# A long S4 and expert-layer kernel on one core: whole rows in one stage of the taps' transform, one product on another engine, and later transposes

## The chip, the cores and the metric

The kernel runs on one core of a Trainium2 chip. The metric is the device time of one execution in microseconds (us). Several executions are timed; one more is recorded by the hardware profiler, and all rows of the profile are from that one.

## The reference

The input x has 2048 rows of 576 channels. The output mixes two branches with a gate for each row:

```python
g = sigmoid((x * gate_w).sum(-1, keepdims=True))
return g * a + (1 - g) * b
# a: K = einsum(C, exp(dt*A*l), dt*B).real      128 states for each of 576 channels
#    a = irfft(rfft(pad(x)) * rfft(pad(K)))[:2048] + x * Dskip
# b: q = x . w_q (32 heads);  s1 = q1 . k1,  s2 = q2 . k2  (64 keys each)
#    the best 2 of each, the best 2 of their 4 sums, softmax -> weights p of 2 experts e for each head
#    b = sum over heads and experts of p * gelu(x . u[e]) * v[e]     (4096 experts)
```

Branch a is a long convolution, done by Fourier transforms; its "taps" are K. Branch b is a layer of experts chosen by product keys.

## The kernel before, in words

One Python program writes the instructions of all engines. While it writes, it keeps a clock of its own with a cost for each instruction; pieces of work are generators that wait on that clock ("ready", "need") and are resumed by a queue ("spawn", "pump"). So the order of the instructions on each engine is fixed when the program is built. It follows from the costs and from the order in which the generators become ready.

TensorE (PE) has two long kinds of work, drawn by the main loop from two lists: 128 "s" groups (scores of one part of the heads `c` for one tile `t` of 128 rows; named s5_0 and so on) and 128 "a" groups (x . u for part `c`; named a6_1_0). Each fills one PSUM bank. A group is written in one of two ways. In `halved` it is 27 matmuls on 64 rows of the array, the upper half rows first and the lower ones later in the same bank; `row_slot` writes one upper half of a group beside one lower half of an earlier group, and the two run side by side. In `triple` it is 14 matmuls on all 128 rows. `start_group` chooses; before, it takes `triple` only if the quota of score banks, `caps["sc"]`, is under 4.

The eight PSUM banks are shared by tags with quotas: "sc" for the groups, "wb" and "kb" for all else. `quota(...)` sets them at each stage.

Between the groups come the stages of the convolution. The first part makes the taps and stores them (`k_gen`, `k_store`, to k_d in HBM). When the last are stored, `freq` starts. It loads the tables tk and the stored taps (ksb, four DMAs), and then does, in this order:

- `k_stage1`: 32 steps, k1_0 to k1_31. Each has two banks (k1_w_0, k1_w_1) of 288 columns, two copies to k1o (four buffers) and one store to sk_d. Before, each bank is 4 half matmuls.
- beside it `v_norm` (loads vn in quads, products on GpSimd, sums of squares vj on ScalarE; at its end a small matmul pvn) and `gating(c)` for the parts of the heads (the softmax weights; tiles ggu, ggd, ggi, ggib; results in vals).
- `products`: 36 steps that load ui and ki back from su_d and sk_d, transform them (matmuls pr, pi), multiply them (tt, vf on VectorE and GpSimd), transform back (pv, vo) and store.
- at the end of `gating(7)` the transposes tr0 to tr15 of vals; then the one-hot matrices and sums S (`prep`), the table vhl of the experts' v, and the output stage, matmuls o.

wn and wb are the small sums and products that build the next part's key weights. Nearly all DMAs are issued by SyncE (SP), in the order in which they are written. In the profile nearly all instructions of an engine have one line (L216 for matmuls, L136 for the other engines, L207 for DMAs), so tiles tell them apart.

Of the kernel before, what the change touches and what calls it, by code (L numbers as in the profile page):

```python
# [140 lines left out]
def body(ctx: ExitStack, tc: tile.TileContext, xT, au, par, logdt, dskip, gatew, wq, kT, uT, vv,  # L141
# [5 lines left out]
    clock = [0.0]  # L147
# [106 lines left out]
                    g["then"]()  # L254

    chained = [False]

    def total(p, cols):

# [752 lines left out]
    def k_store(c, kb):  # L1012
        yield from ready(kb)
        yield from need("ko")
        take("ko", "ko")
        ko = kg.tile([128, 2, 2 * NI * R2], F16, name="ko", tag="ko", bufs=1)
        kq = kb.rearrange("p (c i q) -> p q c i", c=2, i=NI)
        kz = ko.rearrange("p z (q c i) -> p z q c i", c=2, i=NI)
        S.activation(kz[:, 0], kq, AF.Copy)
        yield from ready(ko)  # L1020
        V.tensor_sub(kz[:, 1], kq, kz[:, 0])
        free("kb", ko, of=kb)
        yield from ready(ko)
        kstored[0] += 2
        dma(k_d[c].rearrange("p z m q -> p z (m q)"), ko)
        free("ko", k_d)
        if kstored[0] == NCK:
            while uf != 0:
                yield 0.3
            KG.__exit__(None, None, None)  # L1030
            quota(sc=5, wb=4, kb=0, raw=2)
            spawn(freq())


# [78 lines left out]
    def gating(c):  # L1113

        while taken[c] < 4 or not ff:
            yield 0.5
        vv_ = vals[:, :, 8 * c:8 * c + 8].rearrange("p t (h s) k -> p t h s k", s=2)
        ii = idx[:, :, 8 * c:8 * c + 8].rearrange("p t (h s) k -> p t h s k", s=2)
        tl = lambda nm, *z: ff.tile([128, NT, 4, *z], F32, tag="gg" + nm, name=f"gg{nm}{c}")
        a0, a1, b0, b1 = vv_[:, :, :, 0, 0], vv_[:, :, :, 0, 1], vv_[:, :, :, 1, 0], vv_[:, :, :, 1, 1]  # L1120
        u, w, s, d = tl("u"), tl("w"), tl("s"), tl("d")
        i1, i2, ib = tl("i1", 2), tl("i2", 2), tl("ib", 2)
        G.tensor_add(u, a0, b1)
        G.tensor_add(w, a1, b0)
        G.tensor_add(d, a0, b0)
        yield from ready(u, w)
        V.tensor_tensor(out=s, in0=u, in1=w, op=OP.is_ge)
        V.tensor_tensor(out=u, in0=u, in1=w, op=OP.max)
        yield from ready(u, d)
        G.tensor_sub(d, u, d)  # L1130
        db = d.rearrange("p (b t) h -> p b (t h)", b=4)
        G.tensor_mul(db, db, i_x[:, :, None].to_broadcast([128, 4, 16]))
        dx = d.rearrange("p t (x y) -> p t x y", x=2)
        G.tensor_mul(dx, dx, invW[:, None, 2 * c:2 * c + 2, None].to_broadcast([128, NT, 2, 2]))
        yield from ready(d)
        S.activation(d, d, AF.Exp)
        yield 1
        G.tensor_sub(w, ii[:, :, :, 1, 1], ii[:, :, :, 1, 0])
        G.tensor_mul(w, w, s)
        G.tensor_add(i2[:, :, :, 1], ii[:, :, :, 1, 0], w)  # L1140
        yield 2
        G.tensor_sub(w, ii[:, :, :, 0, 0], ii[:, :, :, 0, 1])
        G.tensor_mul(w, w, s)
        G.tensor_add(i1[:, :, :, 1], ii[:, :, :, 0, 1], w)
        S.activation(i1[:, :, :, 0], ii[:, :, :, 0, 0], AF.Copy)
        S.activation(i2[:, :, :, 0], ii[:, :, :, 1, 0], AF.Copy)
        yield from ready(i1, i2, d)
        V.tensor_scalar(ib, i2, 0.5, -0.25, op0=OP.mult, op1=OP.add)
        V.tensor_scalar(ib, ib, MAGIC, MAGIC, op0=OP.add, op1=OP.subtract)
        V.scalar_tensor_tensor(i1, i2, 64.0, i1, op0=OP.mult, op1=OP.add)  # L1150
        fl = lambda x: x.rearrange("p t h k -> p t (h k)")
        V.scalar_tensor_tensor(place[0][:, :, 8 * c:8 * c + 8], fl(ib), -128.0, fl(i1), op0=OP.mult, op1=OP.add)
        S.activation(place[1][:, :, 8 * c:8 * c + 8], fl(ib), AF.Copy)
        V.tensor_scalar(u, d, 1.0, None, op0=OP.add)
        V.reciprocal(u, u)
        V.tensor_scalar(u, u, 2.0 ** 14, None, op0=OP.mult)
        pr = prob[:, :, 8 * c:8 * c + 8].rearrange("p t (h k) -> p t h k", k=2)
        yield from ready(u)
        S.activation(pr[:, :, :, 0], u, AF.Copy)
        G.tensor_mul(pr[:, :, :, 1], u, d)  # L1160
        if c < 7:
            spawn(gating(c + 1))
            return
        gated.append(1)
        yield from ready(vals)
        for t in range(NT):
            yield from need("wb")
            p = bank("wb", f"tr{t}")
            for r, x, i in ((0, place[0][:, t], identb), (1, place[1][:, t], identb), (2, prob[:, t], ident)):
                for hh in range(2):  # L1170
                    mm(p[64 * hh:64 * hh + 64, 64 * r:64 * r + 64], x, i[:, 64 * hh:64 * hh + 64], True, True,
                       0.12 if r == 2 else 0.04)
            spawn(turned(t, p))
            del p
# [91 lines left out]
    def k_stage1(ksb, fk, tabs):  # L1266
        enter, leave, count = ring(3)

        def tail(w, o, pbs, gs):
            while not all(g["done"] for g in gs):  # L1270
                yield 0.2
            yield from ready(*pbs)
            for hh in range(2):
                copy(o[:, 288 * hh:288 * hh + 288], pbs[hh][:, :288])
                free("wb", o, of=pbs[hh])
            yield from ready(o)
            dma(pair_rows(sk_d, w), o)
            leave(w)

        for w in range(32):  # L1280
            tkt = tabs[w // 16]
            yield from ready(tkt, ksb)
            yield from enter()
            o = fk.tile([128, D], F32, tag="s1o", name=f"k1o{w}", bufs=4)
            pbs, gs = [], []
            yield from need("wb", 2)
            for hh in range(2):
                pb = bank("wb", f"k1_{w}_{hh}")
                pbs.append(pb)
                gs.append(rows(*([(pb[:, :288], tkt[h:h + 64, w % 16, n],  # L1290
                                   ksb[h:h + 64, 2 * hh:2 * hh + 2, :, w, :].rearrange("p j c i -> p (j c) i"),
                                   h == 0 and n == 0, h == 64 and n == 1) for n in range(2)] for h in (0, 64)), first=True))
            spawn(tail(w, o, pbs, gs))
            del pb, pbs
        while count() < 32:
            yield 0.5
# [102 lines left out]
    def freq():  # L1399
        nonlocal ff, ab, iota_a, iota_b  # L1400
        ff = FG.__enter__()
        wrems.append(ff.tile([128, 2, 512], F16, name="wrem3"))
        ksb = KS.__enter__().tile([128, 4, NCK // 2, 32, 2 * NI], F16, name="ksb")
        fk = FK.__enter__()
        tabs = [fk.tile([128, 16, 2, 128], F16, tag="tk", name=f"tk{w0}", bufs=2) for w0 in (0, 16)]
        for w0, tkt in zip((0, 16), tabs):
            dma(tkt, tk_d[:, w0:w0 + 16, :])
        for j in range(4):
            while wire[0] > clock[0] + 2:
                yield 0.3  # L1410
            dma(ksb[:, j].rearrange("p c w i -> p c (w i)"),
                k_d[:, 32 * j:32 * j + 32].rearrange("c l z m n -> (l z m) c n"))
        spawn(v_norm(), 4)
        spawn(gating(0), 20)
        yield from k_stage1(ksb, fk, tabs)
        FK.__exit__(None, None, None)
        KS.__exit__(None, None, None)
        v_pool(0, 3)
        spawn(v_work())
        fp = FP.__enter__()  # L1420
        quota(sc=4, wb=5)
        yield 3
        spawn(prep(0))
        yield from products(fp)
        FP.__exit__(None, None, None)
        quota(sc=4, wb=4)
        ab = ctx.enter_context(tc.tile_pool(name="ab", bufs=1, side="right"))
        iota_a = ab.tile([128, 128, 2], F16, name="iota_a")
        iota_b = ab.tile([128, 64, 2], F16, name="iota_b")
        V.tensor_copy(iota_a, cst[:, 384:512, None].to_broadcast([128, 128, 2]))  # L1430
        V.tensor_copy(iota_b, cst[:, 512:576, None].to_broadcast([128, 64, 2]))
        iotas.append(1)
        v_pool(3, 5)
        while not gated or not gates:
            yield 0.5
        FG.__exit__(None, None, None)
        WJ.__exit__(None, None, None)
        v_pool(5, 8)
        shut.append(1)
# [447 lines left out]
    def start_group(g):  # L1887

        x = xb[tb_of(g)]
        if len(g) == 2:  # L1890
            c, t = g
# [21 lines left out]
                spawn(act_post(c, tb, j, pb))  # L1913
                used(("u", c), ("x", tb))
        parity[0] = tb_of(g) % 2
        if caps["sc"] < 4:
            while upper or lower:
                row_slot()
            chained[0] = False
# [120 lines left out]
```

## Time and profile before

| | us |
|---|---|
| median of 3 runs | 1452.51 |
| lowest to highest | 1450.69 to 1454.05 |
| profiled execution | 1452.08 |
| its span | 1450.3 |
| PE busy in the span | 1421.3 (98%) |
| VectorE (DVE) busy | 1192.9 (82%) |
| ScalarE (ACT) busy | 831.2 (57%) |
| GpSimd (POOL) busy | 478.1 (33%) |

The page's first part gives busy time by engine. A window is a stretch of the span with the busy time of each engine in it. A row of the waits names the engine and tile that waited, what released it, the time in total, how often, and the longest wait. In a timeline a row is one instruction or several alike (xN), with its start, its length, and in brackets the idle time before it. In the shapes, 64\*128 is a matmul on half the array's rows, 128\*128 on all.

### The profile page before, as it was taken

What the parts mean: (1) busy time and instruction counts of PE and PEld (TensorE: products, weight loads), DVE (VectorE), ACT (ScalarE), POOL (GpSimd) and SP (SyncE); (2) the same over time, 40 slices, a digit from 0 to 9 for tenths busy, and PEclk for the clock granted to TensorE, in tenths of its full rate; (3) what the DMA queues carried; (4) which work ended last, traced back from release to release, by engine and by line L of the source; (5) the groups of instructions that cost most, each with busy time, mean ns of one, the idle gap of its engine ahead of it and who ended that gap; (6) DMA issues with size and microseconds to landing.
All of it is one profiled execution on the core that took longest, in us unless ns stands there. A gap on an engine that the chain in (4) does not pass through costs nothing.

```text
span 1450.3 us, 43981 instructions
## 1 busy us (share of the span) xinstructions
PE 1421.3 (98%) x17654; PEld 904.7 (62%) x17654; DVE 1192.9 (82%) x4596; ACT 831.2 (57%) x1445; POOL 478.1 (33%) x488
## 2 busy tenths in 40 slices
PE   7999999999999999999999999999999999999998
PEld 3465567554565665455654444446888788888887
DVE  5887699889889988777789987688988889889870
ACT  6547887987888887664656665563423422332230
POOL 0443265552572663530557899400000000000000
PEclk9999999999999999999999999999999999999999
DMA  9333543343351331238785788687342432541410
GB/s 315 117 110 99 167 134 111 99 129 109 111 157 47 120 104 46 78 125 269 252 274 168 258 275 305 211 269 235 112 137 82 155 120 71 174 129 68 144 52 17
DMA packets 134380, 215.89 MB, mean 149 GB/s; under 512 B 10912, under 2 KB 79904, under 8 KB 127776
## 3 DMA queue, kind: packets, MB, share of 16 engines
q1 hardware_dynamic: 134080, 213.01, 45.3%
q8 instruction: 138, 2.26, 0.7%
q14 instruction: 66, 0.54, 0.1%
q10 hardware_dynamic: 96, 0.07, 0.0%
HBM read 141.74 MB, written 71.30 MB: 147 GB/s over the span
## 4 chain that ended last, share of the span: by engine, by line
PE 90%; DMA 4%; DVE 4%; ACT 1%; issue 1%; SPq 0%; POOL 0%; ACTq 0%; DVEq 0%; POOLq 0%
PE o L216 26%; PE a L216 25%; PE s L216 23%; PE S L216 4%; PE kb L216 2%; PE pr L216 2%; PE wb L216 2%; DMA wq<-in_wq_dram 1%; PE kP L216 1%; PE y L216 1%; DVE i L136 1%; PE pv L216 1%; PE u L216 1%; DVE m L136 1%; DMA ki<-sk_d 1%
## 5 line engine op out<-in xcount | busy, mean ns | idle before, releaser
L216 PE MATMUL s<-whl,xb 64*128 64x512 f16 x3072 | 468.9, 377 | 0.6 <-ACT k1o L136 0.4
L216 PE MATMUL a<-xb,uhl 64*128 64x512 f16 (+1 forms) x3024 | 455.4, 376 | 0.5 <-DVE go L136 0.2
L216 PE MATMUL o<-vhl,wh 128*128 128x288 f16 x3072 | 387.5, 286 | 0.0
L216 PEld LDWEIGHTS <-wh 128*128 128x128 f16 x3072 | 295.8, 98 | 76.1 <-issue 3.7
L216 PEld LDWEIGHTS <-xb 64*128 64x128 f16 x3456 | 227.8, 94 | 165.7 <-issue 14.5
L216 PEld LDWEIGHTS <-uhl 64*128 64x128 f16 (+1 forms) x3024 | 196.3, 94 | 164.9 <-issue 7.4
L136 ACT ACTIVATE wh<-gl,s_wg 128x1024 f16<-128x1024 f32 x64 | 68.8, 1137 | 180.2 <-DVE gl L136 180.2
L136 POOL TENSOR_TENSOR CS<-CS,ex 128x512 f32<-128x512 f32 x72 | 90.7, 1293 | 167.1 <-DVE ex L136 167.1
L136 DVE TENSOR_TENSOR gl<-S,gl 128x256 f32<-128x256 f32 x256 | 90.9, 416 | 48.5 <-PE S L216 26.2
L216 PE MATMUL s<-wrem,xb 64*128 64x512 f16 x384 | 122.1, 376 | 0.0
L216 PE MATMUL a<-xb,wrem 64*128 64x512 f16 (+1 forms) x380 | 120.0, 376 | 0.0
L136 ACT ACTIVATE go<-a,i_a 128x512 f32<-128x512 f32 x99 | 67.6, 684 | 85.7 <-PE a L216 61.4
L136 DVE FIND_INDEX8 i<-m,s 128x8 uint32<-128x64 f32 x520 | 104.9, 223 | 0.0
L136 POOL TENSOR_TENSOR e<-aN,rt 128x512 f32<-128x512 f32 x72 | 84.0, 1186 | 47.1 <-PE kb L216 47.0
L136 DVE FIND_INDEX8 i<-m,sx 128x8 uint32<-128x64 f32 x504 | 99.4, 218 | 0.0
L136 DVE MAX8 m<-s 128x8 f32<-128x64 f32 x520 | 74.4, 215 | 27.0 <-PE s L216 22.8
L136 ACT ACTIVATE gl<-gl 128x1024 f32<-128x1024 f32 x64 | 63.1, 1046 | 47.0 <-DMA gl<-g_d 47.0
L136 DVE TENSOR_TENSOR Bg<-Be,vals 128x1024 f16<-128x1024 f16 x128 | 82.8, 688 | 2.2
L136 DVE SCALAR_TENSOR_TENSOR wh<-gl,s_wg,wh 128x1024 f16<-128x1024 f32 x64 | 78.5, 1279 | 0.9 <-ACT wh L136 0.9
L136 ACT ACTIVATE CS<-CS 128x1024 f32<-128x1024 f32 x72 | 74.6, 1049 | 6.3 <-DVE CS L136 6.1
L136 DVE TENSOR_TENSOR A<-iota_a,vals 128x2048 f16<-128x2048 f16 x64 | 77.8, 1216 | 0.0
L136 DVE MAX8 m<-sx 128x8 f32<-128x64 f32 x504 | 69.4, 209 | 5.4 <-ACT sx L136 5.1
(206 smaller groups left out, 2360.8 us busy)
## 6 DMA issues: line engine op xcount, KB each, us to landing
g_d<-go SPq DMA_DIRECT2D x128, 256.0 KB, 2.6
gl<-g_d SPq DMA_DIRECT2D x32, 1024.0 KB, 7.0
wq<-in_wq_dram SPq DMA_DIRECT2D x16, 1152.0 KB, 6.0
su_d<-us SPq DMA_DIRECT2D x32, 288.0 KB, 2.6
sk_d<-k1o SPq DMA_DIRECT2D x32, 288.0 KB, 2.7
ui<-su_d SPq DMA_DIRECT2D x16, 576.0 KB, 4.1
ki<-sk_d SPq DMA_DIRECT2D x16, 576.0 KB, 5.8
vn<-in_vv_dram SPq DMA_DIRECT2D x32, 288.0 KB, 4.5
```

Of the source, the lines that this page charges most:

```text
L136: return f(*a, **k)
L216: return T.matmul(o, l, r, start=start, stop=stop)
```

## The change

It has three parts. In the taps' first stage, `start_group` writes whole-row groups and `k_stage1` writes two whole matmuls for a bank in place of four halves; "phase" tells where the program is, and the quota of score banks is 4 there, not 5. In `gating(7)` the last product goes to VectorE; the other parts' stays on GpSimd. And the transposes start to be written once the program's clock is 2 us past the point at which vals is ready.

```diff
     chained = [False]
+    phase = ["taps"]
...
-            quota(sc=5, wb=4, kb=0, raw=2)
+            quota(sc=4, wb=4, kb=0, raw=2)
+            phase[0] = "k1"
             spawn(freq())
...
-        G.tensor_mul(pr[:, :, :, 1], u, d)
+        (V if c == 7 else G).tensor_mul(pr[:, :, :, 1], u, d)
...
-        yield from ready(vals)
+        yield from ready(vals, late=2.0)
...
                 pbs.append(pb)
+                if not chained[0]:
+                    for n in range(2):
+                        mm(pb[:, :288], tkt[:, w % 16, n], ksb[:, 2 * hh:2 * hh + 2, :, w, :].rearrange("p j c i -> p (j c) i"),
+                           n == 0, n == 1)
+                    continue
...
         quota(sc=4, wb=5)
+        phase[0] = "products"
...
         quota(sc=4, wb=4)
+        phase[0] = "last"
...
-        if caps["sc"] < 4:
+        if clock[0] < 0 or phase[0] in ("k1",):
             while upper or lower:
                 row_slot()
             chained[0] = False
```

In `start_group` the lines that follow (`triple`, `then`, return) stay. `chained` also decides how the wn sums are written (`total`): whole or halved. Since the order follows from costs, all engines' order changes from here on.

On PE, at the first step of the stage, before: k is k1_0, s_7 and s_8 are groups s5_7 and s5_8, each weight load ahead of its matmul. One upper and one lower half alternate.

```order
11332 L216 MATMUL s_7_11590<-whl_10645,xb_146 128x512
11333 L216 LDWEIGHTS tk_11205
11334 L216 MATMUL k_0_1_11717<-ksb,tk_11205 128x288
11335 L216 LDWEIGHTS xb_146
11336 L216 MATMUL s_7_11590<-whl_10645,xb_146 128x512
11337 L216 LDWEIGHTS tk_11205
11338 L216 MATMUL k_0_1_11717<-ksb,tk_11205 128x288
```

The same place on PE now. The eight matmuls of k1_0 (two banks of two halves each, upper and lower) are four, and stand together.

```order
11114 L216 MATMUL s_7_11585<-whl_10645,xb_146 128x512
11115 L216 LDWEIGHTS tk_11205
11116 L216 MATMUL k_0_0_11596<-ksb,tk_11205 128x288
11117 L216 LDWEIGHTS tk_11205
11118 L216 MATMUL k_0_0_11596<-ksb,tk_11205 128x288
11119 L216 LDWEIGHTS tk_11205
11120 L216 MATMUL k_0_1_11599<-ksb,tk_11205 128x288
11121 L216 LDWEIGHTS tk_11205
11122 L216 MATMUL k_0_1_11599<-ksb,tk_11205 128x288
11123 L216 LDWEIGHTS xb_146
```

What moved: 15 s groups, s5_0 to s5_14, and all of k1 are whole now, and bank 0 of a step comes before bank 1. Further on, pr0 stands after s5_15, s6_0 and s6_4, and no longer after s6_1, s6_5, the uppers of s6_2 and wb7_0.

On SP, the end of the stage before (sk_d is a store of the stage, vn a quad of v_norm's loads, wq the next weights, ui and ki the loads of the first products):

```order
258 L207 DMA vn_12786<-in_au_dram 32x576 x4
259 L207 DMA sk_d<-k1o_12708 32x4x576
260 L207 DMA wq_0_12839<-in_wq_dram 128x2304
261 L207 DMA sk_d<-k1o_12741 32x4x576
262 L207 DMA vn_12884<-in_au_dram 32x576 x4
263 L207 DMA sk_d<-k1o_12769 32x4x576
264 L207 DMA ui_12961<-su_d 128x1152
265 L207 DMA ki_12962<-sk_d 128x1152
```

The end of the stage on SP now:

```order
255 L207 DMA sk_d<-k1o_12216 32x4x576
256 L207 DMA sk_d<-k1o_12229 32x4x576
257 L207 DMA vn_12291<-in_au_dram 32x576 x4
258 L207 DMA sk_d<-k1o_12247 32x4x576
259 L207 DMA ui_12345<-su_d 128x1152
260 L207 DMA ki_12346<-sk_d 128x1152
261 L207 DMA ui_12349<-su_d 128x1152
262 L207 DMA ki_12350<-sk_d 128x1152
263 L207 DMA vn_12353<-in_au_dram 32x576 x4
264 L207 DMA wq_0_12415<-in_wq_dram 128x2304
```

What moved: eight vn quads, not twelve, stand between the first and the last store, and the wq load stands behind the first two pairs of ui and ki.

On VectorE, the end of gating 7 and the first results of the transposes before (vhl is a step of the experts' table, vo a copy of a product's result):

```order
972 L136 TENSOR_SCALAR ggu_15729<-ggu_15729 128x64
973 L136 COPY vo_16092<-pv_0_16093 128x128
974 L136 SCALAR_TENSOR_TENSOR vhl_12897<-vhl_12898,sci,vhl_12897 128x576 x2
975 L136 COPY vo_16092<-pv_0_16176 128x256
976 L136 SCALAR_TENSOR_TENSOR vhl_12897<-vhl_12898,sci,vhl_12897 128x576 x2
977 L136 SCALAR_TENSOR_TENSOR vhl_12898<-vhl_12899,sci,vhl_12898 128x576 x2
978 L136 TENSOR_TENSOR vals<-tr_16268,vals 128x64
```

The same piece of VectorE now:

```order
965 L136 TENSOR_SCALAR sc<-pvn 128x1
966 L136 TENSOR_SCALAR sci<-sc 128x1
967 L136 TENSOR_SCALAR sci<-sci 128x1 x2
968 L136 TENSOR_SCALAR ggib_15480<-ggi_15479 128x128
...
974 L136 TENSOR_SCALAR ggu_15474<-ggu_15474 128x64
975 L136 CAST iota_a<-cst 128x256
976 L136 CAST iota_b<-cst 128x128
977 L136 TENSOR_TENSOR vals<-ggu_15474,ggd_15477 128x16x4
978 L136 TENSOR_TENSOR vals<-tr_15892,vals 128x64
```

What moved: pvn's scale now comes directly ahead of gating 7 (before it stood among the products, ahead of their last copies), the product and the iota casts are between gating and the transposes, and the vhl steps come after the first transposes. On PE pvn now stands behind the last product pv_35, and 57 half matmuls of a groups lie between pvn and tr0. On ScalarE a vhl step stands between the copies of tr0 and tr1. On PE the blocks S15_0 to S15_2 all come ahead of the first o matmul; before, S15_2 came after it.

## The prediction

> **What bounds the kernel now.** I read the page first, then the windows by stage, then what the TensorE (PE) waits for. The page gives the length and PE's share, and one group from which a price comes:
>
> ```profile
> span 1450.3 us, 43981 instructions
> ...
> PE 1421.3 (98%) x17654; PEld 904.7 (62%) x17654; DVE 1192.9 (82%) x4596; ACT 831.2 (57%) x1445; POOL 478.1 (33%) x488
> ...
> L216 PE MATMUL o<-vhl,wh 128*128 128x288 f16 x3072 | 387.5, 286 | 0.0
> ```
>
> PE is busy for 98% of the span. The change can therefore win little by giving PE less work elsewhere; it can win the last idle stretches of PE, or lose by opening new ones. The windows show where they lie: the columns are length, then busy time of PE, PEld, DVE, ACT and POOL, the granted clock and the DMA share.
>
> ```profile
> 651.00:685.10 34.10, 31.68 (x399) 16.74 (x399) 24.58 (x177) 14.75 (x31) 0.00 (x0) 1.00 0.92 282
> 685.10:735.50 50.40, 47.14 (x516) 35.15 (x518) 36.77 (x250) 31.87 (x100) 28.16 (x51) 0.97 0.74 242
> 735.50:748.50 13.00, 11.65 (x157) 8.50 (x152) 12.69 (x107) 6.27 (x19) 6.26 (x14) 1.00 0.82 268
> 748.50:894.50 146.00, 143.24 (x1793) 68.75 (x1791) 131.01 (x804) 91.09 (x256) 121.79 (x151) 1.00 0.74 250
> 894.50:919.50 25.00, 24.35 (x297) 11.33 (x295) 19.33 (x37) 16.32 (x41) 24.06 (x29) 1.00 0.81 283
> 919.50:994.70 75.20, 75.20 (x843) 36.88 (x840) 56.57 (x97) 42.47 (x71) 3.31 (x3) 1.00 0.70 230
> 994.70:1450.30 455.60, 451.96 (x5249) 365.30 (x5248) 368.33 (x612) 134.77 (x137) 0.00 (x0) 1.00 0.35 112
> ```
>
> The second row is the first stage of the taps' transform (k1), the fourth and fifth the products, the last the output. From 651 to 919.5 PE is idle for 34.10 + 50.40 + 13.00 + 146.00 + 25.00 less 31.68 + 47.14 + 11.65 + 143.24 + 24.35, which is 10.4 us. That is the pool for this change. PE's waits name the pieces (total, times, longest):
>
> ```profile
> PE k L216 <- ACT k1o L136: 2.8, 4, 1.1
> PE k L216 <- DVE m L136: 2.5, 1, 2.5
> PE pr L216 <- DMA ki<-sk_d: 1.5, 1, 1.5
> PE wn L216 <- ACT wj L136: 1.4, 2, 0.9
> PE wn L216 <- ACT tt L136: 1.1, 1, 1.1
> ```
>
> **Whole rows cost nearly what halves cost.** Two pieces of PE's timeline: a run of half matmuls (two rows that follow one another) and a run of whole ones.
>
> ```profile
> 951.65 2.32 PE L216 MATMUL a<-xb,uhl 64*128 64x512 f16 x20
> 953.80 0.38 PE L216 MATMUL a<-xb,wrem 64*128 64x512 f16 x1
> ...
> 23.65 1.03 PE L216 MATMUL a<-xb,wrem 128*128 128x512 f16 x4
> 24.51 1.03 PE L216 MATMUL a<-xb,uhl 128*128 128x512 f16 x4
> ```
>
> Twenty halves start over 953.80 - 951.65 = 2.15 us, two in 0.215 us. Four whole ones take 24.51 - 23.65 = 0.86 us, one in 0.215. A group is 27 halves, 13.5 x 0.215 = 2.90 us, or 14 whole, 3.01 us. Fifteen groups change: 15 x 0.11 = 1.6 us more. An o matmul of the k1 shape takes 387.5 / 3072 = 0.126 us, so the 128 whole k1 matmuls are 16.1 us. This work is not new time by itself, since what ends the stage is another matter: the chain through the store.
>
> TensorEngine Tiling (Array Packing) of the Trainium skill, Key Properties, says that a change of tiling mode drains the engine. By that the whole rows would add drains where the halves end and begin again; the rows above show no price for one, and the number of places at which the mode changes after the stage hardly differs (83 against 85), so I add nothing.
>
> **Term 1: the stage and the chain to the first products.** PE's timeline at its start and end:
>
> ```profile
> 656.77 2.33 PE L216 MATMUL s<-whl,xb 64*128 64x512 f16 x20
> ...
> 685.15 0.40 PE L216 MATMUL k<-ksb,tk 64*128 64x288 f16 x1 [2.48 <-DVE m L136]
> ...
> 745.93 2.32 PE L216 MATMUL wb<-kt,wq 128*64 128x64 f32 x72
> ...
> 748.54 0.43 PE L216 MATMUL pr<-ui,cst 64*64 64x256 f32 x2
> ...
> 750.76 0.43 PE L216 MATMUL pr<-ki,cst 64*64 64x256 f32 x2 [1.45 <-DMA ki<-sk_d]
> ```
>
> The first k1 matmul waits 2.48 us. The releaser is given as DVE, but I put it down to the last ksb load. In the new order eight whole s groups and two wb blocks (with their wn sums, about 2.5 us each) stand between the last a6 half and k1. From 656.77 on the halves in the first row are of s alone, so the a6 group before them is done near 657: 657 + 8 x 3.01 + 2 x 2.5 = 686, after that load. So the wait goes, and nothing replaces it. Six s groups lie among the 32 k1 steps: 686 + 16.1 + 6 x 3.01 = 720 for the last k1 if nothing holds it. Then come s5_11 whole (3.0), about 36 more slots of s work (7.8), and pr0, so PE is at the ki part of pr0 at about 733.
>
> To compare with 750.76: three groups of the next head's scores and one wb block move behind pr0. That is 85 halves (85 x 0.1075 = 9.1 us) and the wb row's 2.32, together 11.5 us of work. The same point of work is 750.76 - 11.5 = 739.3. PE alone would gain 6 us.
>
> The store is slower. SP's timeline (start, length) and SP's own waits from 689 to 740:
>
> ```profile
> 689.15 0.59 SPq L207 DMA_DIRECT2D sk_d<-k1o  x1
> 690.22 1.72 SPq L207 DMA_DIRECT2D vn<-in_au_dram  x4
> ...
> 736.81 2.24 SPq L207 DMA_DIRECT2D vn<-in_au_dram  x4
> 739.16 0.52 SPq L207 DMA_DIRECT2D sk_d<-k1o  x1
> 744.16 0.35 SPq L207 DMA_DIRECT2D ui<-su_d  x1
> 744.55 0.43 SPq L207 DMA_DIRECT2D ki<-sk_d  x1
> ```
>
> ```profile
> SPq L207 <- ACT k1o L136: 8.2, 14, 2.7
> SPq L207 <- ACT vj L136: 2.9, 7, 0.6
> ```
>
> SP issues 32 stores, 12 vn quads and one wq load in 50.5 us; 8.2 of these it waits for ACT's copy of a k1 result, so PE and SP set the pace by turns. The other side of that is ACT's wait on stores that have not landed (tile k1o), the source of PE's 2.8 us:
>
> ```profile
>   DMA sk_d<-k1o: 6.2, 9
> ...
> sk_d<-k1o SPq DMA_DIRECT2D x32, 288.0 KB, 2.7
> ```
>
> In the new order eight quads, not twelve, stand between the first and the last store, and the wq load comes later. A store is taken at 0.62 us and a quad at 2.1 to 2.2 (first and last of the twelve above): 32 x 0.62 + 8 x 2.1 = 36.6 us, against PE's 34. SP becomes the slower, by little. The first store goes out near 688, the last at 688 + 36.6 - 0.6 = 724, or 726 with some waiting for vn buffers. The old last store landed just before 744.16 (SP held ui0 until then), 4.9 us after its issue; the median is 2.7. So ui0 goes at 726.7 to 730.9, ki0 0.4 later, and ki0 took 750.76 - 744.55 = 6.2 us to land: 733.3 to 737.5 against 739.3. Gain 1.8 to 6.0; the middle, **-3.8**, is taken. The lower bound is PE's own 6; on the other side, if every k1 step kept the old pace, 0 to +0.5 (the whole-row groups).
>
> **Term 2: the clock.** Windows around the first k1 and around the wait for ki:
>
> ```profile
> 685.00:688.00 3.00, 2.85 (x18) 1.88 (x20) 2.39 (x18) 0.00 (x0) 0.84 (x1) 0.50 0.42 121
> ...
> 750.00:755.00 5.00, 4.24 (x50) 1.91 (x50) 3.42 (x22) 1.00 (x3) 0.80 (x3) 1.00 0.78 246
> ```
>
> After 2.48 us of idle PE the granted clock was 0.50 for some 3.4 us, which cost 1.7; after 1.45 us it stayed 1.00. The first goes with its wait (that is inside term 1). By term 1 PE waits for ki between nothing and 4 us (733 against 733.3 to 737.5), and that may bring one back: 0 to +1.7, I take **+0.6**, a third of it. TensorE: Matmul & The Clock Gate of the Trainium skill, What's actually happening, has the gate halve the clock after an idle window of about 3.4 us; by that alone 2.48 us would not have been enough and this term would be near nothing. The trace disagrees, and the sum goes by the trace.
>
> **Term 3: wn sums.** wn7_0 and wn7_1 waited 1.4 (ACT wj) and 1.1 (ACT tt). The first now stands behind pr0, and its wait lay ahead of the ki wait anyway. The second may lose its 1.1 or keep it and find 0.5 more: -1.1 to +0.5, taken **-0.9**.
>
> **Term 4: the last head's gating and the transposes.** DVE and POOL rows of the gating, then the tile vhl:
>
> ```profile
> 905.53 0.22 DVE L136 TENSOR_SCALAR ggib<-ggi 128x128 f32<-128x128 f32 x1
> ...
> 909.25 0.49 DVE L136 TENSOR_SCALAR ggu<-ggu 128x64 f32<-128x64 f32 x1
> ```
>
> ```profile
> 916.64 0.84 POOL L136 TENSOR_TENSOR vals<-ggu,ggd 128x64 f32<-128x64 f32 x1
> ```
>
> ```profile
>   DMA vhl<-in_vv_dram: 5.9, 1
> ```
>
> POOL's product waited from 909.74 until 916.64 behind other POOL work; on DVE it follows at once, and POOL loses 0.84. But gating 7 is now behind pvn on DVE, and pvn behind the last products on PE. From pvn to the first transpose DVE needs about 0.8 for pvn's scale, 4.2 (905.53 to 909.74), iota casts 0.5 and the product, at most 0.84: 5.5 to 6.3. PE has 57 halves there, 57 x 0.1075 = 6.1. The product therefore costs nothing while DVE is free; without the cover it costs up to its 0.84. Between the first and second transpose ACT does a vhl step, which in the old trace waited 5.9 us for its load. Bounds: 0, with all of it covered, to +3.5, half of that 5.9 and of the 1.1 by which the gating could pass its cover (6.3 + 0.84 less 6.1); taken **+0.9**, near the covered end, since the old stretch from 919.5 has no idle PE with vhl steps in it. POOL's shorter end is worth nothing, since the last products now stand ahead of the transposes and PE is not idle for them. The later transposes (late=2.0) only place them later in PE's order; their matmuls are the same.
>
> **Term 5: output.** Three S blocks now come before the first o matmul: the old rows show no PE idle in the 75.20 us ahead of the output, with the S blocks in it. Bounds 0 and +2, the latter one cold clock of 1.7 and a little waiting; taken **+0.2**, near the row. The rest of the output stage (451.96 of 455.60 busy) does not change.
>
> Sum: -3.8 + 0.6 - 0.9 + 0.9 + 0.2 = **-3.0**. The profiled execution took 1452.08 us (span 1450.3), which is 0.4 under the median of 1452.51, inside its spread of 1450.69 to 1454.05. From the median: **1449.5 us**.
>
> **Rivals.** A, SP does not set the pace and PE runs the stage through: term 1 is -6.0, terms 2, 4 and 5 are 0, term 3 -1.1, so -7.1: 1445.4. For it: SP waits 8.2 us for copies now, so its own issue work is less than 50.5. Against it: 36.6 against 34.
>
> B, slower: ACT stands at the vhl step behind the first transpose until its load lands. The transposes' banks (four) fill, PE waits in order, and all that follows moves. The price is the 5.9 of the vhl row, and the 1.1 of a gating past its cover: 7 in place of 0.9. Sum -3.8 + 0.6 - 0.9 + 0.2 + 7 = +3.1: 1455.6, and with the small gain of term 1 (1.8) 1457.6. It decides once the load lands over 4 us after the first transpose. Against it: 75.20 of 75.20 busy in the old stretch, with a vhl step already among the transposes.
>
> C, the change does not do what it says: the chain of store and load is as late as before, counted in work, so that the stage's gain turns into a longer wait for ki and a cold clock. Term 1 is -1.8, term 2 +1.7, the others as above: -1.8 + 1.7 - 0.9 + 0.9 + 0.2 = +0.1, so 1452.6.
>
> **How the numbers follow.** What a measurement of this kernel can tell is about 0.2%, 2.9 us. Forecast 0.45 (its own range -4.8 to -0.5, of it 0.24 beyond -2.9), A 0.18, B 0.25 (0.24 slower), C 0.12 (0.10 within, 0.02 slower). Faster 0.24 + 0.18 = 0.42; same 0.21 + 0.10 + 0.01 = 0.32; slower 0.26. The range goes from a little below A to B's upper price: 1444.5 to 1457.5.
>
> **What would show it.** Right: no PE wait at the first k1 and clock 1.00 there; last store near 724 to 726; one wait at pr's ki of up to 4 us; tr without a wait over 1 us. Wrong: PE waits of several us at tr (B), no wait at ki (A), or the last store beyond 728 (C). Waits in the products would mean that a stage I took as unchanged has moved.

## The result: slower by 0.5%, and the profile after

The changed kernel takes 1458.47 us (median of 6 runs, 1456.52 to 1462.28), the kernel before 1451.51 us (6 runs). The ratio is 1.0047, with a 95% interval of 1.0035 to 1.0059: about 7 us more, where 3 us less was forecast. The profiled execution is the slowest of the six (1462.28, span 1460.5). About 2.8 us of its excess lie ahead of anything that the change touches: the last matmul of the taps (kb) ends at 653.77, in the kernel before at 651.00. So the two traces are compared from there on.

First the windows of the kernel before and then those of the changed kernel: from the end of kb to the first pr, from there to the first transpose, and from the end of kb to the last o matmul. The columns are as in the prediction.

```profile
651.00:748.54 97.54, 90.50 (x1069) 60.42 (x1069) 74.09 (x532) 52.93 (x149) 34.42 (x65) 0.98 0.81 259
748.54:919.51 170.97, 167.56 (x2089) 80.04 (x2087) 150.31 (x840) 107.37 (x296) 145.86 (x179) 1.00 0.75 254
651.00:1446.66 795.66, 785.21 (x9240) 542.64 (x9240) 648.77 (x2078) 337.53 (x650) 183.58 (x246) 1.00 0.52 172
```

```profile
653.77:739.48 85.71, 81.63 (x581) 42.91 (x581) 60.76 (x429) 44.19 (x122) 24.12 (x45) 1.00 0.83 271
739.48:922.52 183.04, 180.34 (x2258) 86.81 (x2257) 159.50 (x937) 116.64 (x324) 154.90 (x200) 0.99 0.72 242
653.77:1456.86 803.09, 790.13 (x8913) 533.71 (x8913) 646.66 (x2078) 343.38 (x657) 179.02 (x245) 0.99 0.52 171
```

By the last rows, 803.09 - 795.66 = 7.4 us more. PE is idle for 803.09 - 790.13 = 13.0 us in place of 10.4, and busy for 4.9 us more. The stage itself (first rows) is not where it was lost: 97.54 less the 11.5 us of work that moved behind pr0 is 86.0, against 85.71.

PE's waits in the changed kernel name the new place:

```profile
PE tr L216 <- DVE vals L136: 5.8, 1, 5.8
...
PE k L216 <- ACT k1o L136: 2.8, 3, 1.7
PE wn L216 <- ACT tt L136: 2.6, 2, 2.4
PE k L216 <- DVE m L136: 0.9, 1, 0.9
```

The wait for ki (1.5 before) is gone, and at the first k1 step 0.9 is left of 2.5. New are 5.8 us at the first transpose and 2.4 at wn7_1. The timelines around the transposes, first VectorE's, then SP's:

```profile
919.10 0.20 DVE L136 TENSOR_SCALAR ggu<-ggu 128x64 f32<-128x64 f32 x1
927.87 0.29 DVE L136 CAST iota_a<-cst 128x256 f16<-128x256 f32 x1 [8.58 <-DMA g_d<-go]
928.08 0.22 DVE L136 CAST iota_b<-cst 128x128 f16<-128x128 f32 x1
928.21 0.26 DVE L136 TENSOR_TENSOR vals<-ggu,ggd 128x64 f32<-128x64 f32 x1
```

```profile
916.48 1.48 SPq L207 DMA_DIRECT2D vhl<-in_vv_dram  x2
918.07 0.44 SPq L207 DMA_DIRECT2D z_d<-vo  x1
```

VectorE has finished gating 7 but for the product at 919.3 and then stands for 8.58 us at the iota cast. The product, which needs nothing more, is behind it in VectorE's order, and the rest of tr0's matmuls are behind the product. In the program the cast's tile comes from a pool that opens when the products' pool closes; so it can be given memory of vo15, which the last store to z_d still reads. (The trace shows no addresses.) That store goes out at 918.07, behind two vhl loads of 1152 KB, and takes 9.6 us to land (tile z_d, this store alone):

```profile
DMA to landing us min/median/max: 9.6/9.6/9.6
```

918.07 + 9.6 is 927.7, and the cast starts at 927.87. The profile puts the wait down to a store of g_d; that the store to z_d sets it was tested (below). The clock then adds its part:

```profile
924.00:927.00 3.00, 0.00 (x0) 0.00 (x0) 0.00 (x0) 0.00 (x0) 0.00 (x0) 0.75 1.02 372
927.00:930.00 3.00, 1.38 (x28) 1.41 (x28) 0.83 (x4) 0.86 (x2) 0.00 (x0) 0.50 0.85 202
930.00:933.00 3.00, 3.00 (x38) 1.62 (x35) 1.81 (x7) 2.96 (x9) 0.00 (x0) 0.61 0.88 331
```

The granted clock is low for about 3.7 us after PE starts again, which costs some 1.9 us. Together 7.7 us.

### The profile page after: what moved, and what is told of

Same layout as the page of the kernel before. It is cut to its first block, busy times and chain, and to the rows that moved or that the text cites. A ratio compares the mean times of both kernels' runs of the same rounds, so it can differ in the third digit from the quotient of the medians.

```text
span 1460.5 us, 43313 instructions
## 1 busy us (share of the span) xinstructions
PE 1427.5 (98%) x17325; PEld 893.5 (61%) x17327; DVE 1190.9 (82%) x4596; ACT 837.3 (57%) x1452; POOL 473.5 (32%) x487
## 4 chain that ended last, share of the span: by engine, by line
PE 87%; DMA 6%; DVE 3%; SPq 2%; issue 1%; ACT 1%; POOL 0%; DVEq 0%; ACTq 0%; POOLq 0%
PE a L216 26%; PE o L216 24%; PE s L216 21%; PE S L216 4%; PE kb L216 2%; SPq L207 2%; PE pr L216 2%; PE wb L216 2%; PE kP L216 1%; PE y L216 1%; PE pv L216 1%; DMA sk_d<-k1o 1%; DMA ki<-sk_d 1%; DMA ksb<-k_d 1%; PE u L216 1%
## 5 line engine op out<-in xcount | busy, mean ns | idle before, releaser
L216 PE MATMUL s<-whl,xb 64*128 64x512 f16 (+1 forms) x2892 | 457.0, 378 | 0.2
L216 PEld LDWEIGHTS <-xb 64*128 64x128 f16 (+1 forms) x3261 | 214.8, 94 | 177.6 <-issue 18.0
L216 PE MATMUL s<-wrem,xb 64*128 64x512 f16 (+1 forms) x369 | 116.9, 380 | 0.0
L136 DVE FIND_INDEX8 i<-m,sx 128x8 uint32<-128x64 f32 x552 | 108.7, 216 | 0.0
L136 DVE FIND_INDEX8 i<-m,s 128x8 uint32<-128x64 f32 x472 | 95.0, 219 | 0.0
L136 DVE MAX8 m<-s 128x8 f32<-128x64 f32 x472 | 67.2, 212 | 27.7 <-PE s L216 24.1
L136 DVE MAX8 m<-sx 128x8 f32<-128x64 f32 x552 | 75.9, 208 | 5.6 <-ACT sx L136 5.3
```

What stands on the lines that cost most here:

```text
L136: return f(*a, **k)
L216: return T.matmul(o, l, r, start=start, stop=stop)
```

## The experiments

All ratios are to runs of the kernel before on the same chip; different runs can come from different chips. Where two of these runs differ by 2 us or less, the intervals of their ratios touch, so such a difference is a hint and no more.

**The casts out of the way.** The two casts go to GpSimd; the product stays on VectorE, and PE's order is that of the changed kernel.

```diff
-        V.tensor_copy(iota_a, cst[:, 384:512, None].to_broadcast([128, 128, 2]))
-        V.tensor_copy(iota_b, cst[:, 512:576, None].to_broadcast([128, 64, 2]))
+        G.tensor_copy(iota_a, cst[:, 384:512, None].to_broadcast([128, 128, 2]))
+        G.tensor_copy(iota_b, cst[:, 512:576, None].to_broadcast([128, 64, 2]))
```

> The changed kernel with one edit: the two iota casts go to GpSimd. TensorE's order is the changed kernel's, instruction by instruction. Theory: in the changed kernel the last gating product waits on VectorE behind the iota cast, which waits for the memory of the last product's store (z_d); TensorE loses 5.8 us at the transposes and 1.9 more by the clock. Then the wait at tr falls below 1 us, the clock stays 1.00 there, and the time is 7 to 8 us under the changed kernel's, about 1451. Rival (the place of the transposes, or the product's engine, costs the time): the wait stays at 4 us or more and the time within 2 us of the changed kernel's 1458.

Measured: 1450.84 us, ratio 0.9991 (0.9981 to 1.0000), 7.6 us under the changed kernel. PE's waits hold no tr any more; the largest from the stage on are these:

```profile
PE k L216 <- ACT k1o L136: 2.9, 4, 1.3
PE wn L216 <- ACT tt L136: 1.9, 1, 1.9
```

What follows: with PE's order as it was and the product still on VectorE, the loss is gone. It came from the cast ahead of the product, not from the place of the transposes or the product's engine.

**The product back on GpSimd**, with the casts left on VectorE; PE's order is again the changed kernel's.

```diff
-        (V if c == 7 else G).tensor_mul(pr[:, :, :, 1], u, d)
+        G.tensor_mul(pr[:, :, :, 1], u, d)
```

> The changed kernel with the product back on GpSimd; TensorE's order is the changed kernel's. Theory: tr0 is no longer held, since the product doesn't stand behind the casts; but VectorE's subtraction for each transposed tile still does, so the four banks fill and TensorE waits a little later, for the same store: 3 to 5 us of wait, time 1455 to 1458. Rival (the product's engine is the cause): no wait at the transposes, time about 1451.

Measured: 1456.48 us, ratio 1.0026 (1.0014 to 1.0037). PE's wait and VectorE's cast:

```profile
PE tr L216 <- DVE vals L136: 3.7, 1, 3.7
```

```profile
923.44 0.29 DVE L136 CAST iota_a<-cst 128x256 f16<-128x256 f32 x1 [8.49 <-DMA g_d<-go]
```

The cast stands as long as before (8.49 us); the first transposes pass it, and then the banks fill, since VectorE's subtractions are behind it. As expected.

**The store earlier.** In the changed kernel the vhl loads may not go out before the casts are written; the casts stay ahead of the product on VectorE.

```diff
-            while not vnormed or c not in vt or (c < 7 and c + 1 not in vt):
+            while not vnormed or not iotas or c not in vt or (c < 7 and c + 1 not in vt):
```

> The changed kernel with one edit: the loads of the experts' table (vhl) may not be issued before the iota casts are written, so the last store z_d goes out ahead of the two big loads. The casts stay on VectorE, ahead of the gating product. Theory (casts wait for that store, and the store is slow because two loads of 1152 KB go ahead of it): the store lands in 3 to 5 us, not 9.6, the casts wait under 4 us, the wait at tr is under 1 us, 1450 to 1453 us. Rival (the casts wait for something else, or the store is slow by itself): the wait at tr stays at 4 us or more, 1456 to 1459.

Measured: 1450.85 us, ratio 0.9985 (0.9974 to 0.9997). The cast, and the landing of the last store:

```profile
916.36 0.29 DVE L136 CAST iota_a<-cst 128x256 f16<-128x256 f32 x1 [1.34 <-DMA z_d<-vo]
```

```profile
DMA to landing us min/median/max: 3.4/3.4/3.4
```

With nothing large ahead of it the store lands in 3.4 us, not 9.6, the cast waits 1.34 us, and PE has no wait at tr. This shows both links: the cast waits for that store, and the two loads ahead made it late.

**One part at a time.** Parts two and three without the whole rows (product on VectorE, transposes 2 us later):

> The kernel before with the product on VectorE and the transposes 2 us later, without the whole rows. Here the casts stay behind the transposes in VectorE's order. Theory: no wait at the transposes; within 2 us of the kernel before, 1450 to 1453. Rival (these two parts cost the time): 1456 or more.

Measured: 1453.90 us, ratio 1.0014 (1.0005 to 1.0023): no wait at tr, but 2.0 us slower, a little over what was expected. Its profile shows a clock of 0.90 over the 17.6 us just ahead of the first products, about 1.8 us:

```profile
732.70:750.26 17.56, 15.81 (x181) 11.78 (x176) 15.96 (x118) 8.40 (x24) 7.02 (x17) 0.90 0.79 269
```

One profile doesn't say if that is in all of its runs, so the cause of the 2.0 us is left open.

The whole rows alone:

> Whole rows in the stage alone: product on GpSimd, no added 2 us for the transposes. The products end earlier in TensorE's order, so that pvn, gating 7, the casts and the transposes stand in the order of the changed kernel. Theory: the whole-row part by itself puts the casts ahead of the transposes, so there is a wait of 3 to 6 us at the transposes, and 1455 to 1459 us. Rival (the other two parts cost the time): no such wait, and 1448 to 1452.

Measured: 1464.48 us, ratio 1.0086 (1.0073 to 1.0099): more than expected. PE waits at tr, here after six transposes, with the banks full as in the run with the product back on GpSimd, and then in the output stage for one-hot matrices (Bg):

```profile
PE tr L216 <- DVE vals L136: 5.4, 1, 5.4
PE S L216 <- DVE Bg L136: 3.3, 4, 2.0
```

To see if both come from the cast, it went to GpSimd here too:

> Whole rows alone, with the casts on GpSimd: TensorE's order is that of the run with whole rows alone (1464.5 us). Theory (there too, the wait at the transposes, and the later waits of S for the one-hot matrices that follow from it, come from the casts): no wait over 1 us at tr, 1450 to 1454 us. Rival (whole rows alone are slow for another reason, such as the place of the vhl steps): the waits at S stay and it is 1457 or more.

Measured: 1465.08 us, ratio 1.0089 (1.0076 to 1.0103). By its expectation that speaks for the rival. The trace says that the run could not tell: here the product is on GpSimd as well, so the cast was moved into the queue where it does the harm. PE's wait, and GpSimd's queue:

```profile
PE tr L216 <- POOL vals L136: 7.9, 1, 7.9
```

```profile
926.58 0.40 POOL L136 CAST iota_a<-cst 128x256 f16<-128x256 f32 x1 [12.92 <-DMA g_d<-go]
926.91 0.29 POOL L136 CAST iota_b<-cst 128x128 f16<-128x128 f32 x1
927.17 0.32 POOL L136 TENSOR_TENSOR vals<-ggu,ggd 128x64 f32<-128x64 f32 x1
```

So the whole rows alone were run with the other edit, the vhl loads behind the store:

> Whole rows alone, with the vhl loads behind the last store. The run with the casts on GpSimd didn't tell: there the product is on GpSimd too and stood behind the casts again (TensorE waited 7.9 us for it). Here the casts stay on VectorE and find the store landed. Theory (the wait at the transposes of the whole rows alone comes from the store that the casts wait for): no wait over 1 us at tr, and at least 6 us less than 1464.5. The waits at S in the output stage (3.3 us, VectorE standing at gl for a load of g_d) may be another matter: if they follow from the late transposes they go too, 1450 to 1454 us; if they come from the order of the whole rows alone they stay, 1456 to 1459. Rival (neither comes from the store): 1462 or more.

Measured: 1449.49 us, ratio 0.9983 (0.9974 to 0.9992), 15 us under the whole rows alone. The cast waits 1.40 us, and PE waits neither at tr nor at S:

```profile
915.12 0.29 DVE L136 CAST iota_a<-cst 128x256 f16<-128x256 f32 x1 [1.40 <-DMA z_d<-vo]
```

What follows: the whole rows alone put the cast where the transposes wait for it, and without that wait they gain 2.5 us. The other two parts beside them (the run with the store earlier, 0.9985 against 0.9983 here) add no cost that these runs can tell, though alone they were 2.0 us slower.

**The new wait at wn7_1.** On top of the casts on GpSimd, ScalarE's squares for the last weights are written 4 us later.

```diff
-        yield from ready(w)
+        yield from ready(w, late=4.0 if (c, h) == (7, 1) else 0.0)
```

> The changed kernel with the casts on GpSimd, and ScalarE's squares for the last weights' half (wj7_1) written 4 us later, behind the copies tt5 of the products, so that these don't stand behind the load of those weights. Theory (the new wait at wn7_1 is ScalarE standing at wj until the load lands, and it costs 1.9 us and 1.7 more by the clock): no wait over 0.5 us there, the clock stays 1.00 between 760 and 780, 1446.5 to 1448.5 us. Rival (the wait only moves to the next product): 1450 to 1451.5.

Measured: 1449.14 us, ratio 0.9976 (0.9964 to 0.9987), 1.7 us under the run with the casts on GpSimd and between the two expectations. In the stretch around it the clock is full and PE never idle:

```profile
760.00:780.00 20.00, 20.00 (x282) 10.67 (x280) 19.21 (x108) 11.87 (x35) 18.98 (x26) 1.00 0.60 212
```

The wait and the slow clock are gone there, as the theory said, but only about half of the 3.6 us shows in the time, and the two intervals overlap. PE now waits 0.7 us at an earlier wn (751) and 1.1 us for copies at a late product (879); whether these follow from the edit wasn't tried.

**The stage's buffers.** On top of the casts on GpSimd, six k1o buffers; no engine's order changes.

```diff
-            o = fk.tile([128, D], F32, tag="s1o", name=f"k1o{w}", bufs=4)
+            o = fk.tile([128, D], F32, tag="s1o", name=f"k1o{w}", bufs=6)
```

> The changed kernel with the casts on GpSimd (as in the run before of that kind), and six k1o buffers in place of four; all engines have the same order. Theory (SP's queue sets the end of the stage, and TensorE's 2.9 us of waits for k1o copies are only its echo): the waits for k1o shrink below 1.5 us, but the last store goes out within 1 us of the old time, the wait for ki grows by as much, and the time stays within 1 us of 1450.8. Rival (the full buffers hold the stage): the last store goes out 2 to 3 us earlier and the time is 1448 to 1449.

Measured: 1450.02 us, ratio 0.9982 (0.9969 to 0.9995), 0.8 us under the run without them, with overlapping intervals. PE's waits:

```profile
PE pr L216 <- DMA ui<-su_d: 2.8, 1, 2.8
...
PE k L216 <- ACT k1o L136: 0.5, 1, 0.5
```

The waits for k1o fell from 2.9 to 0.5 us, and a wait of 2.8 us for the first ui load took their place. The last store went out at 728.90, 77.1 us after the end of kb, 1.5 earlier than without, so neither side's numbers fit fully. But PE's last k1 step came 4.1 us earlier than without: what PE gained, SP's queue passed on in small part.

**The edits together.** Casts on GpSimd, wj later, six buffers, on the changed kernel:

> The changed kernel with three edits: casts on GpSimd, wj7_1 later, six k1o buffers. Each took a wait away by itself. If the three add, it is 1448 us or less, 0.3% under the kernel before. If the buffers only move the wait to the loads of the first products, as the run with six buffers showed, it is within 1 us of the 1449.1 without them.

Measured: 1448.62 us, ratio 0.9977 (0.9968 to 0.9986): as without the buffers. And the whole rows alone with vhl loads later, wj later and six buffers:

> Whole rows alone with three edits that each took a wait away elsewhere: vhl loads behind the last store, wj7_1 later, six k1o buffers. TensorE's waits from the stage to the output should be the load of ui (2 to 3 us) and little else. If the edits add: 1447 us or less, 0.3% or more under the kernel before. If their effects overlap as in the run with three edits before: within 1 us of 1449.

Measured: 1447.51 us, ratio 0.9973 (0.9963 to 0.9983), a gain of 0.27%, the lowest median of all, between the 1447 of edits that add and the 1448 to 1450 of edits that overlap. What PE still waits for:

```profile
PE pr L216 <- DMA ui<-su_d: 2.0, 1, 2.0
PE pr L216 <- DMA ki<-sk_d: 0.7, 2, 0.4
PE k L216 <- ACT k1o L136: 0.6, 2, 0.3
```

## Why the prediction was wrong

**Term 4, the step that failed.** The prediction counted the chain from pvn to the transposes as "iota casts 0.5": their durations, without asking what a cast waits for. It took +0.9; the runs show 7.6 us (the changed kernel against the casts on GpSimd; by the two ratios 0.0056 x 1452 = 8.1). The kernel before already had the row. This is its tile z_d, under those that waited for it:

```profile
  DVE iota_a L136: 3.5, 1
```

There the cast stood behind all transposes, and PE had no wait at tr. In the new order, which the prediction had before it, the casts stand between gating and the product, so the same wait, now for a store that lands later, is on PE's path. The prediction's bound of +3.5 for term 4 left that out.

**Rival B** named the place (transposes), the sign and nearly the price (7 us against 7.7), but not the mechanism: ScalarE never stood at the vhl step, whose row after tr0 starts without a wait. It was given 0.25.

**Term 1** was mis-sized. From the end of kb to the ki part of pr0 the gain is 1.8 us in the run with the casts on GpSimd, the low end of 1.8 to 6.0, not 3.8. Its ki part:

```profile
738.04 0.43 PE L216 MATMUL pr<-ki,cst 64*64 64x256 f32 x2 [0.43 <-DMA ki<-sk_d]
```

The taps' end is at 651.50 there, so this is 86.5 us after it; the old order gives 99.8 - 11.5 = 88.3. The part that was mis-sized is SP's queue. In the changed kernel:

```profile
689.20 3.93 SPq L207 DMA_DIRECT2D sk_d<-k1o  x2
...
731.92 0.52 SPq L207 DMA_DIRECT2D sk_d<-k1o  x1
734.41 0.35 SPq L207 DMA_DIRECT2D ui<-su_d  x1
734.82 0.42 SPq L207 DMA_DIRECT2D ki<-sk_d  x1
```

The last store goes out 78.2 us after the end of kb, where 73 to 75 was forecast. From the first store to it are 42.7 us, where 36.0 (36.6 - 0.6) was counted from SP's issues. But SP also waited, above all for copies of k1 results:

```profile
SPq L207 <- ACT k1o L136: 4.8, 11, 0.7
SPq L207 <- ACT sx L136: 3.2, 1, 3.2
...
SPq L207 <- DVE k1o L136: 1.4, 2, 0.7
```

The prediction shows such waits for the old stage (8.2 us) and has no term for them in the new one. The shorter landing (2.5 us, not 4.9) gave part of it back. Rival C's sign for the stage, a last store beyond 728 (77 us after the end of kb), came, and its gain of 1.8; its longer wait for ki did not.

PE's own path was nearly right. With six buffers PE is ready for ui at 735.88 - 2.81 = 733.07, which is 81.3 us after the end of kb (651.77 there); the forecast had it at 720 + 3.0 + 7.8 = 730.8, 79.8 after it.

```profile
735.88 0.43 PE L216 MATMUL pr<-ui,cst 64*64 64x256 f32 x2 [2.81 <-DMA ui<-su_d]
```

PE's work did grow by more than the 1.6 us of the whole groups. Some 27 halves at the two ends have no partner: in the changed kernel these are PE's last a6 halves before the whole rows and the first halves of s5_15 behind them.

```profile
656.52 2.75 PE L216 MATMUL a<-xb,uhl 64*128 64x512 f16 x12
659.11 0.59 PE L216 MATMUL a<-xb,wrem 64*128 64x512 f16 x2
...
731.37 2.76 PE L216 MATMUL s<-whl,xb 64*128 64x512 f16 x12
733.97 0.38 PE L216 MATMUL s<-wrem,xb 64*128 64x512 f16 x1
```

Twelve take 659.11 - 656.52 = 2.59 us, 0.216 each, where a pair takes the same time: 27 x 0.108 = 2.9 us more. The prediction doesn't name this price, but has it in its path: the whole rows start at 657 there, and 36 slots lie ahead of pr0. So it does not explain the miss. Nor does its count of eight s groups ahead of k1 and six in the stage (it is seven and a half, and six and a half), since all fifteen are in the path either way.

**Term 3** had the wrong sign. The products came earlier against the load of the last weights, and ScalarE stood at wj with the products' copies behind it:

```profile
767.82 1.16 ACT L136 ACTIVATE wj<-wq 128x1152 bf16<-128x1152 f32 x1 [4.80 <-DMA wq<-in_wq_dram]
```

PE waited 2.4 us, and in the stretch behind it the clock was 0.89 to 0.93 over 20 us. Forecast -0.9; in this profile, with the clock, about +3 (1.3 more waiting than before, and 1.7). The size is not the same in each run: with TensorE's order unchanged the wait was 1.9 us with the casts on GpSimd, 1.0 with the store earlier and 0.4 with the product back on GpSimd, and in the last two the clock stayed at 1.00. The run with wj later got 1.7 us back.

**Term 2**: the wait for ki left no trace on the clock (nothing where +0.6 was taken), but wn7_1 and tr each brought a slow stretch that the prediction didn't price. **Term 5** is small: in the changed kernel PE waits 0.4 us at S.

**The forecast without the one wait.** With it taken away the change measures between -0.8 and -1.1 us by the medians (the two edits of the changed kernel; -2.2 and -1.3 by their ratios) and -2.5 (whole rows alone with the loads later), against a forecast of -3.0. That the last comes near is partly luck: term 1 gave 2.0 of its 3.8 there, and the +1.7 of terms 2, 4 and 5 did not come.

## What to carry to other kernels

When an instruction comes ahead of another in an engine's order, price what it waits for and not how long it runs: a cast of 0.3 us held its queue for 8.6 us because it waited for a store that, by the program's pools, was still reading the memory it writes. Ask this above all of the first write into a pool that has just opened, and count the loads that go ahead of the last store from that memory. Where work moves earlier, check each transfer that kept the old time, since the gain stops at the first that is not there yet.

## What was not expected of the hardware

A store of 576 KB behind two loads of 1152 KB took 9.6 us to land, and 3.4 us when it was issued ahead of them. PE's clock after a wait is not set by the wait's length alone: after 1.92 us (casts on GpSimd, at wn7_1) it was 0.87 over the next 10 us, and after 1.96 us (whole rows alone, at S) it stayed at 1.00.
